# Two small weight loads moved to a second engine's queue, with a new load order and a split copy, in a retention and MLP-mixer kernel

## The chip, the cores and the metric

The kernel runs on one core of a Trainium2 chip. The metric is the device time of one execution in microseconds (us); below, a time is the median of the runs named beside it. Ratios are the mean time of one kernel's fast runs over the mean of the other's fast runs of the same rounds, with a 95% interval, so they are not quite the ratio of the medians that stand beside them. A run is called slow when it took over 1.5% more than the fastest run of the same kernel, and fast otherwise; slow runs are left out of the ratios. Times inside a run count from the start of its profiled span, which is some 2 us shorter than the device time of that execution.

## The reference, cut to what matters

```python
ret = (scale * q @ k.T) * Dmat[None]     # 8 batches, 8 heads, 576 tokens, 64 per head: causal decay
x   = concat_heads(ret @ v)              # [8, 576, 512]
h   = x.transpose(0, 2, 1) @ U @ V       # U [576, 32], V [32, 576]
u   = x + h.transpose(0, 2, 1)
y   = u + relu(u @ w_ch1) @ w_ch2        # 512 -> 2048 -> 512
```

The MLP (the last line) is nearly all of TensorE's work. For the first batch it can only start when attention is done for all tokens, x has gone through U and V, and the first block of `w_ch1` (W1 below) is there as bf16.

## The kernel before

The kernel writes its program with a small planner. Every piece of work is an `op` with engines, an estimated duration, dependencies and a priority. The planner simulates the engines and gives each of them one fixed list of instructions. A load is an op too; the planner estimates its landing with a model of the transfers (`ring`):

```python
            if e == "SP":                                  # an issue on SyncE
                ring = max(ring, t + 700.0) + o.work
                o.vis = ring + self.DMA_LAT                # DMA_LAT = 1700.0: when others may use it
            elif o.work:                                   # an issue on another engine
                ring = max(ring, o.end + 500.0) + o.work
                o.vis = ring + self.DMA_LAT
            else:
                o.vis = o.end + self.LAT[e]
```

The loads of U and V, and their casts to bf16. V [32, 576] is wanted four times, once in each group of 32 partitions, so it is loaded with a broadcast; `VV` also gets a second, shifted copy (`V2`). Staging buffers: `ust`, `vst`.

```python
        def fv(e):
            nc.sync.dma_start(out=vst, in_=moe_V[None, :, :].to_broadcast([4, R, S]))

        ld["lu"] = DMA(1200.0, 500.0, fu, prio=-999.0, after=[ld["consts"]])
        # ...
        ld["lv"] = DMA(500.0, 800.0, fv, prio=-999.0)
        ld["U"] = pl.op("POOL", 250.0, ..., [ld["lu"]], -970.0)
        ld["V"] = pl.op("ACT", 680.0, ..., [ld["lv"]], -935.0, alt=[("DVE", 600.0), ("POOL", 700.0)])
        ld["V2"] = pl.op("POOL", 600.0, ..., [ld["V"]], -150.0)
```

Batch 0's tokens come as two "pairs" of 256 tokens (loads k0 and k2, v0 and v2) and a "half chunk" of 64 tokens (kA, qA, vA). One line fixes the order of the loads on SyncE; the `w` are blocks of the MLP weights:

```python
    line = [...q...] + [load_op(x) for x in ("k0 k2 v0 kA qA v2 vA lu lv w0 w1" + " " + "w2 w3 ...").split()]
```

Where the plan expects TensorE to wait ahead of the MLP, it fills in dummy matmuls on zeros (`ps_big_t<-zer`), which are thrown away.

Of the kernel before, what the change touches and what calls it, by code (L numbers as in the profile page):

```python
# [28 lines left out]
class Plan:  # L29
# [3 lines left out]
    DMA_LAT = 1700.0  # L33
    DMA_AHEAD = 4500.0

# [23 lines left out]
    def run(self, hint=None):  # L59
# [52 lines left out]
        while left:  # L112
            best = None
            for e in engines:
                base = free[e]
                if e == "SP":
                    base = max(base, ring - self.DMA_AHEAD)
                te = INF
                cand = []
                for o, dur in avail[e]:  # L120
                    t = max(base, earliest(o))
                    if t == INF:
                        continue
                    if wary and o.prio > 0 and any(
                        t < (max(hint[h], h.ready)) < t + dur - 150.0 for h in urgent.get(e, ())
                    ):
                        continue
                    cand.append((t, o, dur))
                    te = min(te, t)
                if te == INF:  # L130
                    continue
                t, o, dur = min((c for c in cand if c[0] <= te + self.LOOK.get(e, 1e-6)),
                                key=lambda c: c[1].prio)
                te = t
                k = (te, o.prio)
                if best is None or k < best[0]:
                    best = (k, e, o, dur, te)
# [45 lines left out]
def kernel(  # L183
# [11 lines left out]
    nc = tc.nc  # L195
# [160 lines left out]
    def load_q4(par, prio):  # L356
# [5 lines left out]
        for n, hs in enumerate(halves):  # L362
# [6 lines left out]
            gots.append(DMA(600.0, 3300.0 if par else (1500.0, 2400.0)[1 - n], fn, prio=prio + 0.01 * n,  # L369
# [60 lines left out]
    def load(p, c, prio, early=False, b=None):  # L430
# [17 lines left out]
        for n, (j, dram) in enumerate(((1, k), (0, q), (2, v))):  # L448
# [8 lines left out]
            got[j] = DMA(480.0 if len(pts) == 1 else 900.0, 1220.0 if b is None else 1000.0, fn,  # L457
# [451 lines left out]
    def RV(p, c, prio, q_done=True, b=None, in_sc=False):  # L909
# [49 lines left out]
        def ev_x(e):  # L959
            nc.scalar.activation(out=xs[slot(*xk)][rows].rearrange("p hp hl d -> p hl hp d"),  # L960
                                 in_=po[rows, :, 0:NHP * D].rearrange("p hl (hp d) -> p hl hp d", d=D),
                                 func=AF.Copy)
        if b is None:
            st["x", kb] = [pl.op("DVE", 700.0, ev, [o], prio, rel=[pk])]
        else:
            st["x", kb] = [pl.op("ACT", 610.0, ev_x, [o], prio, rel=[pk])]
# [220 lines left out]
    def load_uv():  # L1187
        gp = nc.gpsimd

        def fu(e):  # L1190
            nc.sync.dma_start(out=ust[:, 0:4, :], in_=moe_U[0:4 * P, :].rearrange("(c p) r -> p c r", p=P))
            nc.sync.dma_start(out=ust[0:HALF, 4, :], in_=moe_U[4 * P:S, :])  # L1192
# [6 lines left out]
        def fv(e):  # L1199
            nc.sync.dma_start(out=vst, in_=moe_V[None, :, :].to_broadcast([4, R, S]))  # L1200

        ld["lu"] = DMA(1200.0, 500.0, fu, prio=-999.0, after=[ld["consts"]])
        ld["lub"] = DMA(1200.0, 500.0, fub, prio=-999.0)
        ld["lv"] = DMA(500.0, 800.0, fv, prio=-999.0)
# [11 lines left out]
    def load_w(prio):  # L1216
        ld["lw"] = []
        for fb in range(4):
            ld["w1", fb] = []
            for hc in range(2):  # L1220
# [8 lines left out]
                o = DMA(450.0, 1400.0 + 350.0 * (fb < 2), fn, prio=prio + fb + hc * 0.1, acq=[key])  # L1229
                ld["lw"].append(o)  # L1230
# [6 lines left out]
        for fb in range(4):  # L1237
            ld["w2", fb] = []
            for hf in range(2):
# [7 lines left out]
                o = DMA(450.0, 1400.0, fn, prio=prio + 10 + fb + hf * 0.1, acq=[key])  # L1247
                ld["lw"].append(o)
# [15 lines left out]
    ld["zero"] = pl.op("POOL", 1600.0, blank, [ld["consts"]], 5.0)  # L1264

    def batch0():
# [4 lines left out]
        for i in range(2):  # L1271
            load_pair(0, i, base + 20 * i, scaled=(2, 2)[i])
# [5 lines left out]
        SC(0, XC, base + 43.0, with_q=False, b=0, apart="sc" == "big")  # L1278
# [92 lines left out]
    line = [ld["q4a", 0], ld["q4", 0]] + [load_op(x) for x in ("k0 k2 v0 kA qA v2 vA lu lv w0 w1" + " " + "w2 w3 w4 w5 w6 w7 w8 w9 q4 w10 w11 kB k5 qB vB v5 k7 w12 w13 w14 w15 lub v7").split()]  # L1371
# [70 lines left out]
```

## Time and profile before

| | before |
|---|---|
| median of 3 runs | 334.8 us (334.13 to 336.29) |
| profiled span, mean TensorE clock | 335.2 us, 0.998 |
| V: issue, landing, first cast | 14.32, 22.36, 22.41 on GpSimd |
| half chunk's k, q and v landed | 13.79, 14.54, 17.47 |
| first real MLP matmul | 24.85 |
| from there to the end | 310.4 us |

The first real MLP matmul is the row `ps_big_t<-uT_t,w_sb` in the timeline. It splits the run into a start, whose limits are loads and hand-overs between engines, and a long part in which TensorE is nearly always at work. The lines that carry this are shown in the prediction.

### The profile page before, as it was taken

Reading aid. Unit: us, or ns where it says so; the run is one execution under the profiler, and the core shown is the slowest. Engines: PE = TensorE matmul, PEld = TensorE weight load, DVE = VectorE, ACT = ScalarE, POOL = GpSimd, SP = SyncE. Lnnn points to the kernel's source line nnn. Section 1 sums busy time; section 2 is a strip of 40 time slices with the busy share of each in tenths; the row PEclk is TensorE's granted clock in tenths of the full one; section 3 lists DMA queues with packets and bytes.
Section 4 is the critical chain, followed back from the end, with each engine's and each line's share of the span. In section 5 each row is a group of like instructions: output and inputs, shape, how many; then the busy total and the mean of one; then the engine's idle time right before and its main releaser. Section 6 shows DMA issues by size and latency. Waiting matters only on the chain.

```text
span 335.2 us, 6423 instructions
## 1 busy us (share of the span) xinstructions
PE 320.2 (96%) x2606; PEld 159.9 (48%) x2649; DVE 154.8 (46%) x243; ACT 134.4 (40%) x240; POOL 87.6 (26%) x123
## 2 busy tenths in 40 slices
PE   8889998999999899999999999999999999999995
PEld 3454445555545444544455454545544444444442
DVE  5843266695755547555467437732533020020011
ACT  4655554468403460166114621364135206404600
POOL 7557447523241213131212321400010010010010
PEclk9999999999999999999999999999999999999999
DMA  8999999998999999999999899942110320011012
GB/s 238 199 277 384 314 222 314 254 243 170 209 227 206 214 195 220 195 230 186 224 218 241 172 208 217 248 73 49 63 65 17 65 93 31 0 65 64 0 47 78
DMA packets 145169, 56.44 MB, mean 168 GB/s; under 512 B 128244, under 2 KB 138484, under 8 KB 145140
## 3 DMA queue, kind: packets, MB, share of 16 engines
q1 hardware_dynamic: 142420, 47.12, 68.1%
q0 software_dynamic: 2720, 8.92, 7.9%
q8 instruction: 20, 0.33, 0.4%
q14 instruction: 9, 0.07, 0.1%
HBM read 37.14 MB, written 9.44 MB: 139 GB/s over the span
## 4 chain that ended last, share of the span: by engine, by line
PE 73%; DMA 12%; SPq 8%; DVE 2%; issue 2%; POOL 1%; ACT 1%
PE ps_big_t L329 63%; DMA q_st<-in_q_dram 5%; DMA st_st<-in_k_dram 5%; SPq L453 4%; PE ps_s L329 4%; PE ps_o L329 3%; PE ps_sc L329 2%; DMA vst<-in_moe_V_dram 2%; SPq L511 1%; DVE ret_t L872 1%; SPq L546 1%; PE ps_big_t L569 1%; SPq L1039 1%; DVE o_sb L1163 1%; SPq L1192 0%
## 5 line engine op out<-in xcount | busy, mean ns | idle before, releaser
L329 PE MATMUL ps_big_t<-uT_t,w_sb 128*128 128x512 bf16 x556 | 131.8, 379 | 1.5 <-POOL w_sb L1233 0.5
L329 PE MATMUL ps_big_t<-w_sb,y_t 128*128 128x512 bf16 x556 | 130.6, 379 | 1.7 <-issue 0.8
L1096 ACT ACTIVATE y_t<-ps_big_t 128x512 bf16<-128x512 f32 x144 | 85.8, 597 | 94.7 <-PE ps_big_t L329 94.0
L329 PEld LDWEIGHTS <-w_sb 128*128 128x128 bf16 x576 | 54.0, 98 | 62.4 <-POOL w_sb L1233 1.1
L329 PEld LDWEIGHTS <-y_t 128*128 128x128 bf16 x576 | 53.9, 98 | 60.6 <-issue 0.8
L1163 DVE TENSOR_TENSOR o_sb<-ps_big_t,u_t 128x512 f32<-128x512 f32 x36 | 24.8, 690 | 82.3 <-PE ps_big_t L329 82.1
L1170 POOL DMA_DIRECT2D out_dram<-o_sb x34 | 19.3, 568 | 136.3 <-DVE o_sb L1163 133.6
L475 POOL TENSOR_TENSOR qkv_t<-st_st,vscale 128x512 bf16<-128x512 f32 (+1 forms) x28 | 29.1, 1040 | 70.2 <-DMA st_st<-in_v_dram 63.8
L872 DVE TENSOR_TENSOR ret_t<-ps_sc,tri 128x1024 bf16<-128x1024 f32 x24 | 29.3, 1220 | 17.1 <-PE ps_sc L329 17.1
L807 ACT ACTIVATE s_sb<-ps_s 128x512 bf16<-128x512 f32 x22 | 13.1, 596 | 55.9 <-PE ps_s L329 55.8
L951 DVE TENSOR_TENSOR x_t<-ps_o,qscale 128x512 bf16<-128x512 f32 x27 | 18.6, 688 | 9.7 <-PE ps_o L329 9.5
L1027 DVE TENSOR_TENSOR u_t<-ps_s,x_t 128x512 bf16<-128x512 f32 x20 | 13.8, 689 | 17.0 <-PE ps_s L329 17.0
L329 PEld LDWEIGHTS <-qkT_t 64*128 64x128 bf16 (+3 forms) x588 | 14.3, 99 | 11.2 <-issue 7.5
L471 DVE CAST qkv_t<-st_st 128x512 bf16<-128x512 f32 x27 | 13.3, 491 | 12.1 <-DMA st_st<-in_k_dram 12.0
L471 DVE CAST qkv_t<-q_st 128x512 bf16<-128x512 f32 x27 | 14.1, 524 | 8.1 <-DMA q_st<-in_q_dram 7.7
L329 PEld LDWEIGHTS <-ret_t 128*128 128x128 bf16 (+2 forms) x336 | 11.4, 97 | 9.3 <-DVE ret_t L872 4.1
L329 PE MATMUL ps_o<-qkv_t,ret_t 128*128 128x64 bf16 (+2 forms) x296 | 11.9, 192 | 2.2 <-DVE ret_t L872 2.1
L329 PE MATMUL ps_sc<-qkT_t 64*128 64x128 bf16 (+2 forms) x336 | 13.3, 215 | 0.7 <-DVE ret_t L872 0.4
L1027 DVE TENSOR_TENSOR u_t<-ps_o,x_t 128x512 bf16<-128x512 f32 x16 | 10.9, 684 | 3.4 <-PE ps_o L329 3.3
L329 PE MATMUL ps_s<-qkv_t 64*64 64x64 bf16 (+2 forms) x188 | 11.3, 206 | 0.4 <-ACT s_sb L678 0.3
L578 ACT ACTIVATE qkT_t<-ps_big_t 128x512 bf16<-128x512 bf16 (+1 forms) x21 | 10.9, 556 | 1.9 <-PE ps_big_t L569 1.5
L329 PEld LDWEIGHTS <-qkv_t 64*64 64x64 bf16 (+2 forms) x220 | 9.0, 105 | 4.9 <-issue 1.5
(112 smaller groups left out, 186.6 us busy)
## 6 DMA issues: line engine op xcount, KB each, us to landing
out_dram<-o_sb POOLq DMA_DIRECT2D x34, 256.0 KB, 3.3
st_st<-in_k_dram SPq DMA_DIRECT2D x24, 256.0 KB, 4.8
q_st<-in_q_dram SPq DMA_DIRECT2D x24, 256.0 KB, 4.9
st_st<-in_v_dram SPq DMA_DIRECT2D x24, 256.0 KB, 5.0
y_t<-in_moe_w_ch_dram SPq DMA_DIRECT2D x10, 512.0 KB, 10.0
wst_t<-in_moe_w_ch_dram SPq DMA_DIRECT2D x6, 512.0 KB, 8.1
st_st<-in_k_dram SPq DMA_DIRECT2D x4, 512.0 KB, 8.7
st_st<-in_v_dram SPq DMA_DIRECT2D x4, 512.0 KB, 8.1
```

The costliest lines, as they stand in the source:

```text
L329: nc.tensor.matmul(*a, skip_group_check=True, **kw)
L453: sent.append(nc.sync.dma_start(out=f[rw, :, :], in_=dram[bb, :, t0:t0 + rw.stop - rw.start, :].rearrange("h s d -> s h d"),))
L471: nc.vector.tensor_copy(**args)
L475: eng.tensor_tensor(out=qkv[slot(*qk)][rows, 2, :, :], in0=at(2)[rows], in1=vscale[rows, c, :, None].to_broadcast([rows.stop - rows.start, ...
L578: nc.scalar.activation(func=AF.Copy, **args)
L807: nc.scalar.activation(out=s_sb[slot(*sk)], in_=ps_s.rearrange("p (a b) -> p a b", b=P), func=AF.Copy)
L872: nc.vector.tensor_tensor(out=ret[slot(*rk)][rows, hl, :, 0:n], in0=bank(hl.start)[rows, None, :, 0:n] if apart else ps_sc[rows, hl, :, 0: ...
L951: nc.vector.tensor_tensor(out=xs[slot(*xk)][rows].rearrange("p hp hl d -> p hl hp d"), in0=po[rows, :, 0:NHP * D].rearrange("p hl (hp d) - ...
L1027: nc.vector.tensor_tensor(out=us[slot(*uk)].rearrange("p (hp hl d) -> p hp hl d", hl=2, d=D), in0=bank().rearrange("p (hp hl d) -> p hp hl ...
L1096: nc.scalar.activation(out=y1s[slot(*yk)][:, f, :], in_=ps_big[slot(*bk)], func=AF.Relu)
L1163: nc.vector.tensor_tensor(out=osb[slot(*ok)], in0=ps_big[slot(*bk)], in1=osb[slot(*ok)] if n else us[slot(*uk)], op=ALU.add)
L1170: eng.dma_start(out=out_flat[row:row + P, :], in_=osb[slot(*ok)])
```

## The change

Its intent: U and V leave SyncE's line of issues and are issued by ScalarE, beside the loads of the first q, so that V lands long before it is wanted; batch 0's k and v pairs all go ahead of the half chunk; the half chunk's output is copied out by ScalarE and VectorE in two halves; GpSimd's zeroing of three tiles moves behind W1's casts. The planner's model of the transfers is adjusted to the new order. The core of the diff:

```diff
-    DMA_LAT = 1700.0
+    DMA_LAT = 2100.0
...
         def fu(e):
-            nc.sync.dma_start(out=ust[:, 0:4, :], in_=...)
-            nc.sync.dma_start(out=ust[0:HALF, 4, :], in_=moe_U[4 * P:S, :])
+            nc.scalar.dma_start(out=ust[:, 0:4, :], in_=...)
+            nc.scalar.dma_start(out=ust[0:HALF, 4, :], in_=moe_U[4 * P:S, :])
...
         def fv(e):
-            nc.sync.dma_start(out=vst, in_=moe_V[None, :, :].to_broadcast([4, R, S]))
-
-        ld["lu"] = DMA(1200.0, 500.0, fu, prio=-999.0, after=[ld["consts"]])
+            nc.scalar.dma_start(out=vst, in_=moe_V[None, :, :].to_broadcast([4, R, S]))
+
+        ld["lu"] = pl.op("ACT", 1300.0, fu, [ld["consts"]], -1999.0, work=200.0)
...
-        ld["lv"] = DMA(500.0, 800.0, fv, prio=-999.0)
+        ld["lv"] = pl.op("ACT", 660.0, fv, (), -1998.0, work=600.0, after=[ld["lu"]])
...
-            st["x", kb] = [pl.op("ACT", 610.0, ev_x, [o], prio, rel=[pk])]
+            insts = []
+            st["x", kb] = [pl.op(e, 390.0, lambda e, hl=hl: ev_x(e, hl, insts), [o], prio, rel=[pk])
+                           for hl, e in enumerate(("ACT", "DVE"))]
...
-    ld["zero"] = pl.op("POOL", 1600.0, blank, [ld["consts"]], 5.0)
+    ld["zero"] = pl.op("POOL", 1600.0, blank, ld["w1", 3], 5.0)
...
-    line = ... "k0 k2 v0 kA qA v2 vA lu lv w0 w1" ...
+    line = ... "k0 k2 v0 v2 kA qA vA w0 w1" ...
```

Cut: a limit on how far SyncE issues ahead (`RING`), names for the weight loads, and two load estimates.

More of the change, by code (lines that the diff above doesn't have):

```diff
@@ L32 @@
     LOOK = {"DVE": 150.0, "ACT": 150.0}
-    DMA_LAT = 1700.0
+    DMA_LAT = 2100.0
     DMA_AHEAD = 4500.0
+    RING = 2900.0
     def __init__(self):
@@ L115, in run @@
                 base = free[e]
-                if e == "SP":
-                    base = max(base, ring - self.DMA_AHEAD)
                 te = INF
@@ L121, in run @@
                     t = max(base, earliest(o))
+                    if e == "SP":
+                        t = max(t, ring - self.DMA_AHEAD if o.name == "w" or ring > 60000.0 else ring + o.work - dur - self.RING)
                     if t == INF:
@@ L368, in fn @@
                 )
-            gots.append(DMA(600.0, 3300.0 if par else (1500.0, 2400.0)[1 - n], fn, prio=prio + 0.01 * n,
+            gots.append(DMA(600.0, 3300.0 if par else (1300.0, 2200.0)[1 - n], fn, prio=prio + 0.01 * n,
                             acq=[] if n else keys))
@@ L456, in fn @@
                     ))
-            got[j] = DMA(480.0 if len(pts) == 1 else 900.0, 1220.0 if b is None else 1000.0, fn,
+            got[j] = DMA(480.0 if len(pts) == 1 else 900.0, 1220.0 if b is None else 1250.0, fn,
                          prio=prio + (0.0, 0.01, 0.5)[n], acq=[] if j == 2 else [home[j]],
@@ L958, in ev, with ev_x @@
             )
-        def ev_x(e):
-            nc.scalar.activation(out=xs[slot(*xk)][rows].rearrange("p hp hl d -> p hl hp d"),
-                                 in_=po[rows, :, 0:NHP * D].rearrange("p hl (hp d) -> p hl hp d", d=D),
-                                 func=AF.Copy)
+        def ev_x(e, hl, insts):
+            args = dict(out=xs[slot(*xk)][rows, :, hl, :],
+                        in_=po[rows, hl, 0:NHP * D].rearrange("p (hp d) -> p hp d", d=D))
+            insts.append(nc.scalar.activation(func=AF.Copy, **args) if e == "ACT" else nc.vector.tensor_copy(**args))
+            if len(insts) == 2:
+                own(insts)
         if b is None:
@@ L1190, in fu @@
         def fu(e):
-            nc.sync.dma_start(out=ust[:, 0:4, :], in_=moe_U[0:4 * P, :].rearrange("(c p) r -> p c r", p=P))
-            nc.sync.dma_start(out=ust[0:HALF, 4, :], in_=moe_U[4 * P:S, :])
+            nc.scalar.dma_start(out=ust[:, 0:4, :], in_=moe_U[0:4 * P, :].rearrange("(c p) r -> p c r", p=P))
+            nc.scalar.dma_start(out=ust[0:HALF, 4, :], in_=moe_U[4 * P:S, :])
         def fub(e):
@@ L1229, in load_w @@
                 o = DMA(450.0, 1400.0 + 350.0 * (fb < 2), fn, prio=prio + fb + hc * 0.1, acq=[key])
+                o.name = "w"
                 ld["lw"].append(o)
@@ L1247, in load_w @@
                 o = DMA(450.0, 1400.0, fn, prio=prio + 10 + fb + hf * 0.1, acq=[key])
+                o.name = "w"
                 ld["lw"].append(o)
@@ L1271, in batch0 @@
         for i in range(2):
-            load_pair(0, i, base + 20 * i, scaled=(2, 2)[i])
+            load_pair(0, i, base + 20 * i, scaled=2)
         load(0, XC, base + 40.0, early=True, b=0)
@@ L1277, in batch0 @@
         t_pe(0, XC, base + 42.0, b=0)
-        SC(0, XC, base + 43.0, with_q=False, b=0, apart="sc" == "big")
+        SC(0, XC, base + 43.0, with_q=False, b=0)
         sp = -4.0
@@ L1370, in load_op @@
         return ld["q4", 1] if x == "q4" else L(x)[0]
-    line = [ld["q4a", 0], ld["q4", 0]] + [load_op(x) for x in ("k0 k2 v0 kA qA v2 vA lu lv w0 w1" + " " + "w2 w3 w4 w5 w6 w7 w8 w9 q4 w10 w11 kB k5 qB vB v5 k7 w12 w13 w14 w15 lub v7").split()]
+    line = [ld["q4a", 0], ld["q4", 0]] + [load_op(x) for x in ("k0 k2 v0 v2 kA qA vA w0 w1" + " " + "w2 w3 w4 w5 w6 w7 w8 w9 q4 w10 w11 kB k5 qB vB v5 k7 w12 w13 w14 w15 lub v7").split()]
     for a, b in zip(line, line[1:]):
```

## The prediction

> **What bounds the kernel now.** I read the page's busy table first, then the chain of work that ended last in order of time, then one-microsecond windows of the first 60 us, then the timeline of the same stretch, and last the DMA records.
>
> ```profile
> PE 320.2 (96%) x2606; PEld 159.9 (48%) x2649; DVE 154.8 (46%) x243; ACT 134.4 (40%) x240; POOL 87.6 (26%) x123
> ```
>
> TensorE is busy for 320.2 of 335.2 us and the change removes none of its real work, so only idle or dummy time of TensorE can be won. Before 24.85 us its busy time is largely dummy matmuls on zeros and small attention pieces; the first real MLP matmul starts at 24.85. The chain leads there:
>
> ```profile
> 12.10 1.00 SPq L1191
> 13.14 1.14 SPq L1192
> 14.32 8.04 DMA vst<-in_moe_V_dram
> 22.41 0.68 POOL VV L1209
> 23.14 0.67 POOL VV L1213
> 23.81 1.00 POOL w_sb L1233
> 24.85 2.76 PE ps_big_t L329 x12
> ...
> 42.90 8.73 DMA st_st<-in_k_dram
> ```
>
> The two U issues hold SyncE's queue for 2.1 us, V takes 8.04 us to land, GpSimd then casts V twice before the first cast of W1, and the first MLP matmul waits for that cast. It looks as if V were the whole startup. The timeline says otherwise:
>
> ```profile
> 20.97 0.59 ACT L960 ACTIVATE x_t<-ps_sc 64x512 bf16<-64x512 f32 x1 [0.25 <-PE ps_sc L329]
> 22.02 0.60 ACT L998 ACTIVATE a_sb<-ps_big_t 128x512 bf16<-128x512 f32 x1 [0.46 <-PE ps_big_t L329]
> 22.41 0.67 POOL L1209 CAST VV<-vst 128x576 bf16<-128x576 f32 x1 [3.21 <-DMA vst<-in_moe_V_dram]
> 23.13 0.38 PE L329 MATMUL ps_big_t<-VV,a_sb 128*128 128x512 bf16 x1 [0.43 <-POOL VV L1209]
> ```
>
> The other operand of the V product, a_sb, is ready at 22.62, against V at 23.08. V costs that path only about 0.46 us: two paths are nearly level. The windows show the third limit, the transfers:
>
> ```profile
> 15.00:16.00 1.00, 0.75 (x33) 0.69 (x33) 0.38 (x1) 0.69 (x2) 0.73 (x1) 1.00 0.86 100
> 16.00:17.00 1.00, 1.00 (x49) 0.79 (x41) 0.64 (x1) 0.82 (x3) 0.59 (x1) 1.00 0.45 81
> 18.00:19.00 1.00, 1.00 (x50) 0.81 (x45) 1.00 (x2) 1.00 (x3) 1.00 (x2) 1.00 0.87 199
> 25.00:26.00 1.00, 1.00 (x6) 0.40 (x5) 0.72 (x2) 0.00 (x0) 0.94 (x1) 1.00 1.05 387
> 50.00:51.00 1.00, 0.60 (x25) 0.54 (x27) 0.97 (x2) 0.00 (x0) 1.00 (x2) 1.00 1.08 367
> 51.00:52.00 1.00, 0.57 (x24) 0.38 (x20) 1.00 (x2) 0.35 (x1) 0.61 (x2) 1.00 1.08 383
> ```
>
> The last two columns are the DMA share and GB/s. From 3 to 42 us the share is about 1 or above except at 15 to 19, around U and V, where 81 to 232 GB/s flow instead of the 387 that W1 gets at 25. In the rows at 50 and 51 TensorE (first pair) is busy for 0.60 and 0.57 of each us: it waits there for batch 1, whose k lands at 51.63 as the chain shows. So the transfer line, not the start at 24.85 alone, decides where TensorE stands at 55 us. Summing TensorE's busy time by 5 us windows, it idles 2.1 us between 40 and 55, and another 1.5 us between 110 and 120.
>
> **What the skill says.** "DMA: Bandwidth & Descriptors", section "Rules for kernel authors", says that a transfer whose outermost dimension is a broadcast of c copies runs on at most c engines. V's is a broadcast of four. The trace agrees: V's 128 packets of 2304 B run from 15.72 to 21.21, about 5.5 us for 288 KB, and its last four semaphore increments come at 21.96 to 22.36 while no others arrive near them. W1's first block shows the same four behind: twelve increments by 21.01, four at 23.28 to 23.52. The same page, "Issuing engines are not separate DMA queues", says that issuing from another engine saves only the issuing time; the transfers share the 16 engines. Its "Queues, rings and completion order" says each engine takes turns between queues packet by packet. Before has a single hardware queue (142420 packets on q1), so no line shows the sharing yet. "PSUM — Partial Sum Buffer", section "PSUM bank collisions raise a hardware error", lets ScalarE and VectorE read different banks together. The half chunk's output lies in two banks, and the trace has such a pair already (18.91 on ScalarE, 19.23 on VectorE).
>
> **The change part by part.**
>
> 1. U and V move to ScalarE's queue. Their issue follows the constants: the last trix activation ends at 3.65. Two U issues at 0.50 and 0.58 (the uncongested pair at 49.2 us) and V at 0.66 end near 5.5. ScalarE has nothing else before 7.62, so nothing waits. SyncE gets back 1.00 + 1.14 + 0.66 = 2.8 us of issuing, which produced the hole at 15 to 17 us. Lost transfer in that hole: (1 - 0.86) + (1 - 0.45) = 0.7 us.
>
> 2. V's bytes don't go away. In packets of 93 ns, as at 16.7 to 17.3 where it ran alone, 32 packets on each of four engines are 3.0 us; at the 178 ns it averaged beside W1 (22.3 us of packets over 128) they are 5.6. U is 576 packets at 15 ns over 16 engines, 0.5 us. Both now lie ahead of k and v on those four engines, and a load is done only when its slowest engine is. I take 2.7 us of delay for batch 0's loads: 3.5 less about 0.8 that another engine was late anyway (k lands at 8.43 where fifteen engines were done at 7.93; v at 12.56 where they were done at 11.75).
>
> 3. Order k k v v. The second v (16.34 before) goes ahead of the half chunk's k and q, whose landings cost 14.54 - 12.56 = 2.0 us: it would land at 14.4 + 2.7 = 17.1. The half chunk's q lands about 2 us after that, at 19.1. From there I add the durations of the same work in before: q scale 1.04, transposes and copy 0.8, scores and mask 1.1, its output matmuls 0.9, copy 0.4, last U product 0.4, and 0.5 of hand-overs = 5.1. So a_sb would start at about 24.2 against 22.02. The first MLP matmul then follows with no wait for V: a_sb 0.60, V product 0.45, copy 0.65, about 0.2 of hand-overs: 26.1 instead of 24.85. With V costing nothing it would be 23.4. I take 25.6 as my middle, as ports and packets may overlap better than a plain sum.
>
> 4. The half chunk's copy in two: 0.59 becomes about 0.4 (the 64x256 pair at 18.91 and 19.23 took 0.36 and 0.43), 0.2 us won; already counted in the 5.1.
>
> 5. The zeroing on GpSimd, 0.95 + 0.52 + 0.52 = 2.0 us at 4.0 to 5.9, moves behind W1. GpSimd can cast q at 4.7 instead of 5.96. That wins 0.4 us on q, but k lands later than q is ready, so nothing is left of it. It later fits GpSimd's idle stretch at 36.8 to 40.6.
>
> 6. The transfer line behind: on the four engines V still stands before W1's first block, so that one is earlier only by the hole, 0.7 us, and by whatever V runs faster than its 5.6 us, at most 2.6. I take 1.2 us. W1's block lands near 22.3 and its cast, with V's casts long done, is ready at 23.4, before it is needed.
>
> **The sum.** The start of the MLP goes from 24.85 to about 25.6 (0.8 later). Batch 1's loads come 1.2 earlier. TensorE had 2.1 us of waiting in 40 to 55; the later start uses up 0.8 of it and the earlier loads remove 1.2, leaving about 0.1. At 55 us TensorE is then about 1.2 us ahead. Behind 55 both TensorE and the transfers have moved by the same 1.2, so most carries through; I take 0.4 off for waits on orders of transfers at 100 to 120 that don't move along. Gain 0.8: 334.8 - 0.8 = 334.0 us.
>
> **Rivals.** (a) V early is nearly free, as the queues interleave: the MLP starts at 23.4 to 24 and the transfers are 2.6 ahead. For it: V's packets took 93 ns alone. Against: packets of 2304 B slowed W1 to 199 GB/s at 18. It would make 332.3. (b) V early holds the four engines for 5.6 us and SyncE, which is held back when any engine is behind (its v issue at 3.40 took 2.66 us), stalls too: the MLP starts at 27.5 or later, past what the 2.1 us of slack absorbs. For it: the spread of V's packets beside other traffic. It would make 336. (c) A new plan: the latency (2100 for 1700) and the ring model change the order of every engine's instructions, so parts after 60 us may move by 1 us either way. For it: the waits at 110 to 120 are for orders (SyncE's transposes and loads behind VectorE). Nothing in the profile gives its sign. (d) All is hidden and the time is the same within 0.3 us: the loads after 60 us have a DMA share above 1 to 200 us.
>
> **Range and chances.** The sum lies between rivals (a) and (b), whose ends are 332.3 and 336.0, and the three runs of before spread by 2.2 us. I take 332.1 to 335.9 for 8 in 10. Two per cent are 6.7 us; the whole removable startup (24.85 to 23.4) plus the waits in 40 to 55 and 110 to 120 is 1.5 + 2.1 + 1.5 = 5.1. So faster by 2% is nearly excluded (0.02), slower takes a broken order (0.02), and 0.96 is left.
>
> **What would show it.** Step 1: a second hardware queue in the table of queues, and no hole at 15 to 17. Step 2: V landing by 9 to 12 us, k and v later than 8.43 and 12.56 by up to 3 us. Step 3: the wait ahead of the first MLP matmul names ScalarE's or VectorE's uT, not GpSimd's w_sb. Step 6: W1's first cast before 23.5 and batch 1's k before 51. It would be wrong if V's landing doesn't delay k at all, or if TensorE still waits 2 us between 40 and 55, or if the difference sits after 100 us.

## The result, and the profile after

| | before | after |
|---|---|---|
| median | 334.91 us (4 runs, 334.13 to 336.29) | 345.07 us (4 runs, 344.51 to 345.76) |
| ratio of the fast runs | | 1.030 [1.026, 1.034]: slower |
| profiled span, clock | 335.2 us, 0.998 | 344.1 us, 0.978 |
| V: issue, landing, first cast | 14.32, 22.36, 22.41 | 8.75, 19.92, 19.95 |
| half chunk's k, q and v landed | 13.79, 14.54, 17.47 | 20.24, 20.95, 21.25 |
| first real MLP matmul | 24.85 | 37.04 |
| from there to the end | 310.4 us | 307.0 us |

The kernel came out about 10 us slower, and the prediction (334.0 us, 332.1 to 335.9, "slower" at 0.02) was wrong. All of the loss is in the start: the first MLP matmul comes 12.2 us later, and 3.4 us of that come back afterwards. They come from waits of TensorE that before had: between the first MLP matmul and 62 us it idles 2.2 us before and 0.7 after, between 100 and 150 us 2.4 before and 0.6 after, together 3.3. (Between 62 and 100 us it idles 0.9 us more after, so this account is rough.)

From the page of after, the busy line, two rows of the 40 slices (one digit for 8.6 us, tenths busy or tenths of the clock) and the second hardware queue:

```profile
PE 325.5 (95%) x2614; PEld 162.3 (47%) x2657; DVE 155.0 (45%) x243; ACT 133.3 (39%) x240; POOL 89.1 (26%) x125
...
PE   8559999899999999999999999999999999999995
...
PEclk9659999999999999999999999999999999999999
...
q10 hardware_dynamic: 740, 0.37, 0.6%
```

The second hardware queue, q10, is there with U's and V's 740 packets. TensorE and its clock both dip in the second and third slice (8.6 to 25.8 us), where before has 8 and 8 and a full clock. The same stretch as windows, TensorE's busy time first, then weight loads, VectorE, ScalarE and GpSimd; the last three columns are the granted clock, the DMA share and GB/s. Before:

```profile
10.00:15.00 5.00, 3.92 (x83) 2.07 (x82) 4.52 (x5) 2.70 (x6) 2.92 (x4) 1.00 1.29 212
15.00:20.00 5.00, 4.75 (x174) 3.99 (x174) 2.77 (x5) 3.14 (x7) 3.54 (x4) 1.00 0.85 172
```

After:

```profile
10.00:15.00 5.00, 3.17 (x46) 2.17 (x47) 1.45 (x2) 2.75 (x7) 0.88 (x2) 0.63 1.25 248
15.00:20.00 5.00, 1.31 (x5) 0.35 (x3) 1.33 (x2) 0.06 (x1) 0.00 (x0) 0.50 1.11 202
```

From 15 to 20 us three engines stand still at once: TensorE runs 5 matmuls instead of 174, ScalarE nothing, GpSimd nothing. The transfers don't: their share rose from 0.85 to 1.11, so the hole of before was filled as intended. Something waits, and not for bandwidth. The chain of work that ended last, in order of time (start, duration, what), names it:

```profile
1.86 6.87 DMA st_st<-in_k_dram
8.73 0.02 issue
8.75 11.17 DMA vst<-in_moe_V_dram
19.92 0.02 issue
19.95 0.68 ACT VV L1216
20.63 0.49 ACT qkT_t L579
21.12 0.04 issue
21.17 0.64 PE ps_o L330 x13
```

In before the chain went from V to the MLP directly. Here it goes from V's landing to V's cast on ScalarE, and from there to `qkT_t`, a piece of attention that has nothing to do with V: the copy of the second pair's transposed k. Two things that share only an engine have become a chain. The timeline shows how (start, duration, engine, line, operation; in brackets the idle time before it and what ended it):

```profile
8.75 1.11 ACTq L1205 DMA_DIRECT2D vst<-in_moe_V_dram  x1
...
9.91 1.21 ACT L423 ACTIVATE qkT_t<-ps_sc 128x256 bf16<-128x256 bf16 x4 [6.26 <-DMA ust<-in_moe_U_dram]
...
12.16 0.62 ACT L525 ACTIVATE qkv_t<-st_st 128x512 bf16<-128x512 f32 x1
...
19.95 0.68 ACT L1216 ACTIVATE VV<-vst 128x576 bf16<-128x576 f32 x1 [7.17 <-DMA vst<-in_moe_V_dram]
...
20.69 0.67 POOL L1218 COPY VV<-VV 128x576 bf16<-128x576 bf16 x1 [8.42 <-ACT VV L1216]
...
21.17 0.64 PE L330 MATMUL ps_o<-qkT_t 64*64 64x128 bf16 x16 [4.63 <-ACT qkT_t L579]
...
21.32 3.05 POOL L530 TENSOR_TENSOR qkv_t<-st_st,vs 128x512 bf16<-128x512 f32 x3
```

ScalarE stands for 7.17 us ahead of V's cast, from 12.78; behind it wait the copies of the second pair's transposed k, which TensorE had finished by 15.3. GpSimd stands for 8.42 us ahead of V's second copy, with v's casts (`L530`) behind it, whose first data had landed at 12.89. And the first bracket is a second finding: ScalarE copies the transposed q only at 9.91 (7.62 in before), right after it has issued V. The profile's releaser there (U) is only the last event that it saw; the program's list tells more. ScalarE's instructions in the program's order, with the semaphores they wait for:

```
L1196 DMACopy ust<-in_moe_U_dram 128x4x32 [waits DVE]
L1197 DMACopy ust<-in_moe_U_dram 64x32 [waits DMAHW0]
L1205 DMACopy vst<-in_moe_V_dram 128x1x576 [waits DMAHW2]
L423 Activation qkT_t<-ps_sc 128x256 [waits PE] x4
L525 Activation qkv_t<-st_st 128x512
L579 Activation qkT_t<-ps_big_t 128x512 [waits PE]
L525 Activation qkv_t<-st_st 128x512 [waits DMAHW3]
L1216 Activation VV<-vst 128x576 [waits DMAHW2]
L579 Activation qkT_t<-ps_big_t 128x512 [waits PE] x2
```

The loads of SyncE and ScalarE share eight semaphores (DMAHW0 to 7), and V got the one that the first k was using. So V's *issue* waits until that k has landed: it landed at 8.73 and V was issued at 8.75. The same pair in four of the experiments below: 8.21 and 8.23, 8.12 and 8.14, 8.63 and 8.66, 8.15 and 8.17. An engine that issues a load can be held by another load's landing. (The trace holds the same: V's issue waits for the semaphore that the first k's landing counts up.)

Why is V's cast where it is? Because the planner believed in an early V. Its own figures for after (in us of the plan, whose k0 lands at 8.2 against 8.73 in the trace) and what the trace has:

```
                     plan          trace
V issued             5.69          8.75
V landed            10.99         19.92
V's cast            11.03         19.95
first MLP matmul    24.78         37.04
```

3.1 us of the 8.9 that the landing is late come from the issue, the rest from a flight of 11.17 us where the plan has 5.3.

### The profile page after: what moved, and what is told of

It reads as the page before. It is cut to its first block, busy times and chain, and to the rows that moved or that the text cites. A ratio compares the mean times of both kernels' runs of the same rounds, so it can differ in the third digit from the quotient of the medians.

```text
span 344.1 us, 6434 instructions
## 1 busy us (share of the span) xinstructions
PE 325.5 (95%) x2614; PEld 162.3 (47%) x2657; DVE 155.0 (45%) x243; ACT 133.3 (39%) x240; POOL 89.1 (26%) x125
## 4 chain that ended last, share of the span: by engine, by line
PE 87%; DMA 7%; DVE 2%; issue 1%; SPq 1%; ACT 1%; DVEq 0%
PE ps_big_t L330 72%; PE ps_o L330 5%; PE ps_s L330 5%; PE ps_sc L330 4%; DMA vst<-in_moe_V_dram 3%; DMA st_st<-in_k_dram 2%; DMA q_st<-in_q_dram 2%; PE ps_big_t L570 1%; SPq L1044 1%; DVE o_sb L1168 1%; DVE ret_t L873 1%; DVE ret_t L717 0%; ACT qkT_t L579 0%; SPq L366 0%; PE ps_sc L405 0%
## 5 line engine op out<-in xcount | busy, mean ns | idle before, releaser
L873 DVE TENSOR_TENSOR ret_t<-ps_sc,tri 128x1024 bf16<-128x1024 f32 x24 | 29.3, 1222 | 20.7 <-PE ps_sc L330 20.6
L330 PEld LDWEIGHTS <-qkT_t 64*128 64x128 bf16 (+3 forms) x588 | 15.0, 104 | 16.8 <-issue 7.9
L472 DVE CAST qkv_t<-st_st 128x512 bf16<-128x512 f32 x27 | 14.0, 518 | 4.6 <-DMA st_st<-in_k_dram 4.5
L330 PE MATMUL ps_big_t<-zer 128*128 128x512 bf16 x30 | 11.5, 523 | 1.5 <-DVE zer L279 1.3
```

Of the source, the lines that this page charges most:

```text
L330: nc.tensor.matmul(*a, skip_group_check=True, **kw)
L472: nc.vector.tensor_copy(**args)
L873: nc.vector.tensor_tensor(out=ret[slot(*rk)][rows, hl, :, 0:n], in0=bank(hl.start)[rows, None, :, 0:n] if apart else ps_sc[rows, hl, :, 0: ...
```

## The experiments

Three theories were on the table. **A, order**: V's cast and second copy stand in ScalarE's and GpSimd's lists ahead of work whose data is there, and everything behind them waits for V. **B, engines**: V's broadcast on four of the DMA engines delays every load that also uses those four, the half chunk's above all. **D, clock**: TensorE's halved clock from 11.3 to 24.9 us makes the start slow. The new load order and ScalarE's blocked issue are smaller suspects. "First MLP" below is the time of the first real MLP matmul in the profiled run; the kernels ran on several chips, each beside runs of before on the same chip, whose medians lay between 334.5 and 336.0. Each is compared by its ratio to those.

### V's casts late, all else as in after

```diff
         RV(0, XC, base + 59, q_done=False, b=0, in_sc=True)
+        ld["V"].after.extend(st["x", (XC, 0)])
+        ld["V2"].after.extend(st["x", (XC, 0)])
```

> The changed kernel, with one edit: the program order puts the casts of V behind the half chunk's output instead of ahead of batch 0's second k pair; the load of V stays on ScalarE's queue, at the same place. Theory A (in-order blocking: the 10 us come from ScalarE and GpSimd standing still for V's landing at 19.9, with V's cast ahead of work whose data had landed): ScalarE's 7.2 us wait before L1216 goes, TensorE's pause from 16.5 to 21.2 goes, the first MLP matmul moves from 37.0 to about 28 and the time falls from 345 to about 337. Theory B (transfer contention: V on four engines beside the loads delays k and v, and the cast's place hardly matters): k of the half chunk still lands near 20.2 and the time stays at 342 or more. V should land near 19.9 under both.

Measured: 338.85 us, ratio 1.016 [1.006, 1.026], first MLP at 30.51. V still lands at 19.87 and the half chunk's k at 20.18. The long waits on ScalarE and GpSimd for V are gone and the clock is 1.0 throughout the profiled run. This lies between the two forecasts (337 and 342 or more), nearer to A's. In the first 30 us the order of instructions differs from after's, on all engines but TensorE, in these two casts alone; TensorE's gets a few other dummies. How much comes back depends on how it is counted: 6.2 of 10.2 us by the medians (345.07, 338.85 and 334.91, which come from different sessions), 1.4 of 3.0 per cent by the ratios, 6.5 of 12.2 us by the first MLP matmul. Theory A is about half of the loss, perhaps more. What holds the start now is in the chain that ended last:

```profile
8.23 1.11 ACTq L1205
9.38 1.21 ACT qkT_t L423 x4
...
19.70 1.79 issue
```

It begins with the first k's landing, V's blocked issue on ScalarE and q's copy behind it, at 9.38 (7.62 in before), and goes on through attention to TensorE, which then stops for 1.79 us in the middle of a group of matmuls; for this stop the profile shows no releaser, and its cause stays open. GpSimd does wait 4.7 us for the half chunk's k, but its cast is done by 20.85 and TensorE comes to that k only at 22.01: B is not on this chain.

### V alone back on SyncE; U stays on ScalarE

```diff
-            nc.scalar.dma_start(out=vst, ...)
+            nc.sync.dma_start(out=vst, ...)
-        ld["lv"] = pl.op("ACT", 660.0, fv, (), -1998.0, work=600.0, after=[ld["lu"]])
+        ld["lv"] = DMA(500.0, 800.0, fv, prio=-999.0)
-    "k0 k2 v0 v2 kA qA vA w0 w1"
+    "k0 k2 v0 v2 kA qA vA lv w0 w1"
```

> The changed kernel with V alone back on SyncE's queue, behind the half chunk's v; U stays on ScalarE's queue, and all the rest of the change stays. Theory A and B both expect most of the loss to go, as neither the cast nor the transfer of V is then in the way: half chunk's k lands near 16 instead of 20.2, first MLP matmul near 25, time 334 to 336. Theory C (the new order k k v v, or the new constants of the plan, cost it): time stays above 340. It also shows what U alone costs on ScalarE's queue.

Measured: 336.03 us, ratio 1.006 [0.998, 1.014], first MLP at 26.87, half chunk's k at 16.02, V's cast on VectorE at 21.70. Much as expected (the first MLP 1.9 us later than the 25 that was forecast): with everything else of the change kept, the loss is gone but for what the interval can't tell from zero. The half chunk's k lands 4.2 us earlier than with V in flight beside it (20.18 and 20.24): that is how much B delays this load. It is not what B costs in time, as this edit also ends the blocked issue: ScalarE copies q at 7.30 instead of 9.38. No run separates the two.

### U and V back on SyncE

```diff
-        ld["lu"] = pl.op("ACT", 1300.0, fu, [ld["consts"]], -1999.0, work=200.0)
+        ld["lu"] = DMA(1200.0, 500.0, fu, prio=-999.0, after=[ld["consts"]])
   (V as above; the line "... vA lu lv w0 w1")
```

> The changed kernel with U and V both back on SyncE's queue where they were; order k k v v, half copies, zeroing behind W1 and the plan's constants stay. Theories A and B: 334 to 336, within 0.5% of before, as the remaining parts move nothing on the path. Theory C (those remaining parts cost the 10 us): 343 or more.

Measured: 338.61 us (336.8 to 340.7), ratio 1.013 [1.004, 1.023], first MLP at 30.45. Higher than expected, a miss in part. V lands at 21.77 and its cast was planned on ScalarE ahead of the copies of x, with a wait of 2.3 us: theory A again, smaller. The profiled run also shows something in the clock column of its windows:

```profile
16.00:19.80 3.80, 3.03 (x89) 2.27 (x85) 2.48 (x4) 2.22 (x5) 2.25 (x3) 1.00 1.02 220
19.80:25.00 5.20, 4.70 (x54) 2.37 (x46) 1.28 (x2) 1.18 (x2) 2.39 (x3) 0.50 1.04 335
25.00:30.00 5.00, 5.00 (x32) 2.62 (x30) 0.50 (x2) 1.55 (x3) 3.78 (x5) 0.50 1.05 383
```

TensorE runs at half clock from 19.8 to 30.0 in this run, though after its first matmul it is nowhere idle for over 0.6 us before. That this is the rest of the loss isn't shown: the runs of this kernel with mean clocks 0.985, 1.0, 0.997 and 0.987 took 338.71, 338.51, 336.79 and 340.71 us, so the one at full clock is no faster than the profiled one.

### The move of U and V alone, on before

```diff
 (before, with the changed fu, fv, ld["lu"] and ld["lv"] of the change, and)
-    "k0 k2 v0 kA qA v2 vA lu lv w0 w1"
+    "k0 k2 v0 kA qA v2 vA w0 w1"
```

> The kernel before with the move of U and V to ScalarE's queue alone; order k k v, half chunk, v and all constants as before. Theory A: the plan again believes that V lands early and puts its cast on ScalarE ahead of the half chunk's k, so ScalarE waits some 5 us for V: 341 to 346. Theory B: 341 to 346 too, as the transfers overlap in the same way. Theory C (order or constants are needed for the loss): 334 to 337.

Measured: 337.13 us (335.6 to 340.3), ratio 1.007 [0.998, 1.017]; the profiled run is the slowest, 340.32, with its first MLP at 32.4. A miss: I expected most of the loss. V lands at 18.09 here, and in the plan with before's constants, which puts V's cast later, ScalarE's wait for it is 4.3 us instead of 7.2. It seems that the cost of a misplaced cast depends on how far the list has got when the wait comes; no run varies that alone.

### Dummy matmuls in TensorE's two pauses

```diff
+    warm = {id(tpe[1]): 8, id(scp[2]): 18}     # TensorE's pieces behind the two pauses
...
                 zeros(at + 40.0, o.start - 80.0)
+                for _ in range(warm.get(id(o), 0)):
+                    mm(ps_s, zer[:, 0:P], zer, start=True, stop=True)
```

> The changed kernel with 26 more dummy matmuls on zeros, 8 ahead of the transposes that wait at 9.8 us and 18 ahead of the scores that wait at 16.5 us; nothing else moves. It asks what the halved clock of TensorE (0.5 from 11.3 to 24.9 us) costs by itself. If the halved clock matters (theory D): clock 1.0 through 30 us, first MLP matmul 1.5 to 3 us earlier than 37.0 and the time about 342.5 to 343.5. If it is only a mark of the waiting (theory A alone): clock 1.0, but the first MLP matmul within 0.7 us of 37.0, time 344 to 345.5.

Measured: 345.78 us, ratio 1.033 [1.023, 1.043], first MLP at 38.1. Its windows:

```profile
10.00:15.00 5.00, 4.74 (x60) 2.46 (x59) 2.46 (x4) 2.66 (x7) 0.88 (x2) 1.00 1.25 244
15.00:20.00 5.00, 3.22 (x15) 1.27 (x13) 0.38 (x1) 0.06 (x1) 0.00 (x0) 1.00 1.14 190
20.00:25.00 5.00, 3.84 (x39) 1.69 (x40) 3.05 (x3) 1.60 (x3) 4.31 (x5) 0.57 0.86 277
```

The clock is 1.00 up to 20 us where after has 0.63 and 0.50, and the time is the same within the intervals, a little above both forecasts. D falls for the pauses: the half clock there is a by-product of the waiting. It halved later, from 20.7 to 27.5, which this run didn't prevent.

### V as the very first issue on ScalarE, its casts late

```diff
-        ld["lv"] = pl.op("ACT", 660.0, fv, (), -1998.0, work=600.0, after=[ld["lu"]])
+        ld["lv"] = pl.op("ACT", 660.0, fv, (), -2001.0, work=600.0)
   (and V's casts late, as in the first experiment)
```

> The changed kernel with the load of V as the very first issue on ScalarE's queue (so it meets no earlier load on its semaphore, and flows beside the first q as the change's name says) and the casts of V behind the half chunk's output, as in the run with late casts (338.85, first MLP matmul 30.5, half chunk's k at 20.2). Semaphore theory (E: V's issue at 8.75 waited for the landing of the first k because both use one semaphore): V is issued near 0.8 and lands by 7, and ScalarE copies q near 7.6 to 8 instead of 9.9. If then the half chunk's k lands near 17 and the first MLP matmul is near 27: 335 to 336.5, contention only matters where V collides with the half chunk. If V on four engines delays all behind it wherever it flows (theory B): k of the half chunk still near 19 to 20 and 338 or more.

Measured: 343.38 us, ratio 1.027 [1.019, 1.034], first MLP at 33.84. The chain of waits now begins

```profile
0.81 10.10 DMA vst<-in_moe_V_dram
```

and the DMA records show B directly. A load counts up its semaphore once for each engine that is done. For q's second half twelve of the sixteen counts are in by 7.75 and the last four come at 11.16 to 11.56; for the first k twelve by 10.83, four at 12.76 to 13.11; for the second k twelve by 12.36, four at 14.48 to 14.88. In before q's second half was whole at 6.15. V, alone on four engines, delays these loads on those four by 2 to 4 us, and takes 10 us itself even when it is first. Not all of this run's time is B, though: U's issue (10.99) waited for V's landing (10.91) on a shared semaphore, U landed at 17.90, and its cast stood on GpSimd ahead of the second k's, whose data had been there since 14.88; TensorE waits 1.8 us for that.

### V as four loads of 32 rows, on the kernel with V on SyncE

```diff
-            nc.sync.dma_start(out=vst, in_=moe_V[None, :, :].to_broadcast([4, R, S]))
+            for i in range(4):
+                nc.sync.dma_start(out=vst[32 * i:32 * i + 32, :], in_=moe_V)
```

> The run with V back on SyncE (336.0; V issued at 12.5, landed at 21.7, last four increments of W1's first block 2 us behind) with one edit: V as four loads of 32 rows each in place of one broadcast. Theory B in its narrow form (the broadcast runs on four engines): sixteen engines carry V, it lands within 5 us of its issue, near 18, W1's first block lands near 20.5 instead of 22.8 with its increments together, and all of W1 comes 1.5 to 2 us earlier. The time then falls only if the start of the MLP was waiting for transfers: 334 to 336. Rival: the four issues and their semaphores cost SyncE as much as they win, W1 no earlier than 22.5.

Measured: 336.38 us (one of four runs slow, which is the profiled one), ratio 1.005 [0.995, 1.015]. W1's first block lands at 20.64 (22.78 with the broadcast), its sixteen counts together but one. That block came earlier as expected, but V's last piece landed only at 19.61 (near 18 was expected) and the next blocks of W1 hardly earlier than with the broadcast (23.56 against 24.11, 25.18 against 25.46); the time did not move.

### The old load order in after

```diff
-    "k0 k2 v0 v2 kA qA vA w0 w1"
+    "k0 k2 v0 kA qA v2 vA w0 w1"
```

> The changed kernel with the old order of loads (k k v, half chunk's k and q, then the second v); U and V stay on ScalarE's queue. If the order k k v v is innocent: V's cast still stands ahead of the second k pair's copies on ScalarE, time 343 to 346. If the order matters (the move alone, on before, cost only 2 us): 336 to 340.

Measured: 343.2 us, ratio 1.028 [1.018, 1.038], first MLP at 33.89, ScalarE's wait for V 6.0 us. Beside after's 1.030 the order k k v v costs nothing that can be told from noise. The medians differ by 1.9 us and the first MLP by 3.2, so a cost of that size isn't excluded either.

### V first, as four loads of 32 rows, its casts late

```diff
   (the kernel with V first, and)
-            nc.scalar.dma_start(out=vst, in_=moe_V[None, :, :].to_broadcast([4, R, S]))
+            for i in range(4):
+                nc.scalar.dma_start(out=vst[32 * i:32 * i + 32, :], in_=moe_V)
```

> The run with V issued first (343.4; q's second half late on four engines by 4 us, half chunk's k at 21.8) with one edit: V as four loads of 32 rows in place of the broadcast. Narrow theory B (what hurts the loads is that the broadcast runs on four engines): V lands by 6, q's second half by 7.5 with its increments together, half chunk's k by 17.5, first MLP matmul near 27.5 instead of 33.8, time 335 to 337.5. Rival (any V beside the first loads delays them, as its bytes have to pass): q's second half still after 9 and the time 341 or more.

Measured: 343.86 us, ratio 1.025 [1.020, 1.029], first MLP at 33.44. B's delays are gone: q's second half is whole at 7.31 with its counts together, V's last piece lands at 9.01 in the trace and the half chunk's k at 16.66. The time is a miss all the same. The table of waits says why:

```profile
POOL UU L1211 <- DMA ust<-in_moe_U_dram: 5.1, 1, 5.1
PE ps_big_t L570 <- POOL qkv_t L527: 4.8, 1, 4.8
```

U is now issued behind V's four pieces, at 7.39, because that issue again waits for a semaphore (q's second half, landed at 7.31), and it lands at 13.9; its cast stands in GpSimd's list ahead of the second k pair's (`L527`). GpSimd waits 5.1 us for U, TensorE 4.8 us for GpSimd. The same fault with another tile. So neither this run nor the one with V as four loads on SyncE shows that B cost device time: both took B's delays away and neither became faster (in this one the wait for U may hide it).

### The same four loads, on before

Two kernels: before with V as four loads of 32 rows on SyncE, and before with those four as the first issues on ScalarE (casts where the planner puts them).

```diff
+            for i in range(4):
+                nc.sync.dma_start(out=vst[32 * i:32 * i + 32, :], in_=moe_V)        # first kernel
+                nc.scalar.dma_start(out=vst[32 * i:32 * i + 32, :], in_=moe_V)      # second kernel
```

> The kernel before with one edit: V as four loads of 32 rows on SyncE's queue, at V's old place. From the run with the same edit on V back on SyncE, where W1's first block landed at 20.6 instead of 22.8: W1's first block lands near 21 instead of 23.5, batch 1's k near 49.5 instead of 51.6, and TensorE's 2.2 us of waiting between its first MLP matmul and 62 us shrinks to about 1. The first MLP matmul moves little (24.3 to 24.9), as a_sb is ready only at 22.6. Time 1 to 2.5 us below before. Rival: the semaphores and issues eat it, within 0.3%.

> The kernel before (its order, its constants, U where it was) with V as four loads of 32 rows issued first on ScalarE's queue. What the change wanted, with sixteen engines: V lands by 6, q and k are later by at most 1 us, V's casts are done by 7.5 and W1's first block lands near 21.5. Time 332.5 to 334.5. Rival: ScalarE's four issues (about 1.6 us) delay the constants and V's cast stands ahead of q's copies on ScalarE and GpSimd, so all starts 1 us or more later: 335 to 338.

Measured: the first 336.72 us (333.3 to 340.1, two of six runs slow), ratio 1.002 [0.997, 1.007], the same. A miss: 1 to 2.5 us were to be won. Its profiled run is the fastest of its six, with W1's first block at 20.36, the first MLP at 22.91 and a span of 330.9 us, but the other runs don't follow. The second, a miss too: 339.01 us, ratio 1.010 [1.007, 1.014], first MLP at 29.31: V's cast on ScalarE at 8.79 and its second copy on GpSimd stand ahead of q's casts, and TensorE pauses from 6.71 to 10.83.

### V first in four loads, and U's cast late too

In the kernel with 1.025, one instruction moves: U's cast on GpSimd, from ahead of the second k pair's cast to behind the half chunk's.

```diff
         ld["V2"].after.extend(st["x", (XC, 0)])
+        ld["U"].after.append(st["v", 3])
```

> The kernel with V in four pieces first on ScalarE and V's casts late, and now also U's first cast moved, on GpSimd alone, from ahead of the second k pair's cast to behind the second v pair's and the half chunk's k cast; it is the one instruction that moves. If what was left of the loss there is again a cast placed in an engine's order ahead of work whose data has landed (the in-order theory), the 5.1 us wait of GpSimd and the 4.8 us wait of TensorE for it go, the first MLP matmul comes at 27 to 29 instead of 33.4, and the time is 335 to 338 against 343.9. If an early V costs the time in another way (the transfers, the clock), the first MLP matmul stays above 31.5 and the time at 341 or more. Below 334 would show that the move can be made to win.

Measured: 337.63 us (5 runs), ratio 1.007 [1.002, 1.013], first MLP at 28.49. Both waits are gone, and with them 5 us of the start; the ratio went from 1.025 to 1.007 (each beside before on its own chip). As forecast, and this is A in its purest form: the two traces hold the same instructions in the same order on every engine, but for this one cast. (The two kernels ran on different chips, each beside before.) What ScalarE does early is still held up, as the head of this kernel's chain shows:

```profile
1.84 7.77 DMA vst<-in_moe_V_dram
...
9.63 0.53 ACTq L1197
...
10.20 1.21 ACT qkT_t L423 x4
```

V's third piece landed at 9.61, U's second issue (`L1197`) waited for that semaphore until 9.63, and q's copy on ScalarE, at 7.62 in before, came at 10.20: the blocked issue, once more.

### The rest: without the plan's dummies

That kernel's first MLP is still 3.6 us later than before's. From 12.1 us on its chain has no transfer in it, almost only TensorE's own list, and the plan has put 16 dummies there (6 in the same stretch of before). Is that list what costs the 3.6 us? Three kernels leave out the dummies behind the first pair's: this one, the one with V on SyncE, and before as a control.

```diff
-        for _ in range(min(n, 14)):
-            mm(bank, zer[:, 0:P], zer, start=start, stop=True)
+        for _ in range(min(n, 14, 20 - len(fill))):        # 21 and 22 in the other two
+            fill.append(mm(bank, zer[:, 0:P], zer, start=start, stop=True))
```

> The kernel with V in four pieces first and all casts late, without the 16 dummy matmuls on zeros that its plan places behind the first k pair's transposes (from 12.3 us of its trace). If the rest of the loss is TensorE's own list (16 dummies at 0.22 to 0.38 us), the first MLP matmul comes 2.5 to 3.5 us earlier, at 25 to 26 instead of 28.5, and the time is 333.5 to 336, level with before or a little ahead of it. If the rest is the transfers (the half chunk's q at 18.8 against 14.5), the waits reappear where the dummies were, the first MLP matmul moves by less than 1 us and the time stays near 337. A third way: with the pauses unfilled the granted clock halves for some us, and the time is above 338.

> The kernel with V alone back on SyncE, without the 14 dummies that its plan places from 12.4 us on. Its first MLP matmul was at 26.9 and its time 1.006 of before. If TensorE's list sets it, 24.5 to 25.5 and 333 to 335; but there V's own landing, at 21.7, and its cast come close behind, so less is to be won than in the run with V first: if they set it, 26 or later and 335 to 336.

> Control: before without its last dummies (6 in the trace from 11.6 us on). Its start waits for V and W1's first cast at 22.4 to 24.9, not for TensorE, so nothing should be won: first MLP matmul at 24.5 to 25, time within 0.5% of before. If the time gets worse by more, the dummies keep the clock up there.

Measured: 337.61 us, ratio 1.007 [1.002, 1.012], first MLP at 28.64; 339.74 us, 1.012 [1.007, 1.018], 30.72; 335.71 us, 1.001 [0.996, 1.005], 24.52. The dummies cost nothing: without them TensorE of the first kernel idles 7.0 us before its first MLP matmul instead of 4.1, and starts no earlier. In the first kernel's chain

```profile
4.22 9.72 DMA st_st<-in_v_dram
...
14.09 2.05 POOL qkv_t L530 x2
```

a load is in it again, the first v, which lands at 13.95 against 12.56 in before; the half chunk's k, q and v land at 17.29, 18.26 and 19.04 against 13.79, 14.54 and 17.47. So the rest goes with later loads, as V's, U's and the second v's bytes now lie ahead of the half chunk; how much of it is the blocked ScalarE these runs don't tell. The second kernel, a miss, is slower where its clock halves (from 19.9 to 33.6 in the profiled run): its five runs fall into two with mean clock 1.0 (337.13 and 336.62) and three with 0.975 to 0.978 (339.7 to 341.3). With the dummies its four runs all had 0.998 to 1.0, and without them some runs of the other two kernels too show a lower clock than with them (0.97, in a slow run, and 0.985 are the lowest). The dummies may thus keep the clock up, but the chips differ and no run tests it.

## Why the prediction was wrong

**Step 1 failed: "ScalarE has nothing else before 7.62, so nothing waits."** V's issue was to end near 5.5; it ended at 9.86, because it waited for the first k's semaphore, and ScalarE, which was to copy q at 7.62, stood behind it until 9.91. In after the wait for V hides what this costs; in the run with V's casts late, where that wait is gone, it heads the chain (q's copy 1.8 us late). I had asked what ScalarE does, not what the issue itself may wait for. The second half of the step held: the hole in the transfers at 15 to 20 us is filled.

**The step that is missing: where V's cast stands.** Step 6 says "with V's casts long done" and nothing more. No step asks where the planner would put the casts once it believes V to be early, nor what happens if V is late. The Trainium skill has the fact that decides it: "PSUM — Partial Sum Buffer", section "Engine vs sequencer instructions", says that the queues of ScalarE, VectorE and GpSimd are strictly first in, first out. The trace agrees: ScalarE stands for 7.17 us and GpSimd for 8.42, with work behind them whose data was there by 15.3 and 12.89. The diff has the planner's belief in plain sight: `work=600.0` and a latency of 2.1 us for a load whose flight in before had been 8.04. Moving the two casts gave half of the loss back or somewhat more (338.85 us, ratio 1.016); moving U's cast alone took the other kernel from 1.025 to 1.007. In before the fault couldn't show: V landed at 22.36, and nothing of batch 0's attention was left to stand behind it.

**Step 2 was right in kind and mis-sized.** V's four engines do delay the other loads: 4.2 us for the half chunk's k (20.24 against 16.02 with V on SyncE), where I took 2.7 for batch 0's loads. And it hit other loads than I said. The first v landed only 0.3 us later (12.89 against 12.56), since V was not yet in flight; V "landing by 9 to 12" was 19.92. V's flight is the term that was mis-sized, 10 to 11 us instead of 3.0 to 5.6, and not by the pace of its packets: they took 171 ns on average and ran from 12.69 to 18.90, near to the 5.6. What the step leaves out is the time around them: 3.9 us from the issue to the first packet (1.4 in before) and 1.0 us from the last packet to the landing. With the late issue these make up the delay.

**Step 3** had `a_sb` at about 24.2; it came at 35.30. With V out of the way (V on SyncE) it is 25.13, and with V first and all casts late 26.75, so the sum of durations itself was 1 to 2.5 us short, not 11.

**Steps 4 and 5 held.** The half copies ran at once, both at 34.05, one on each of the two banks, and took 0.38 us on ScalarE and 0.42 on VectorE against 0.59 for the whole; and the zeroing, now at 35.7 to 37.6, shows up in no wait of TensorE. **Step 6** had W1's first block at 22.3, and it landed at 22.54; its cast, predicted ready at 23.4, began only at 27.34, because GpSimd was 7 to 8 us behind in its list. That did no further harm, as the MLP started at 37. The "2.1 us of slack" behind the start, and the 1.5 at 110 to 120, were real: most of the 3.4 us that came back were absorbed there.

**Of the rivals**, (b) named V's hold on the four engines and put the time at 336; the run that has it, and the blocked issue, without the misplaced casts took 338.85. (c), a new plan, was held to 1 us either way "after 60 us"; it was the part that the runs have shown, and it struck before 22 us. The chance of 0.02 for "a broken order" was far too low for a change that lets a planner with wrong constants reorder five engines.

**What stays open.** The sizes of the two kernels with U and V on SyncE or moved alone (ratios 1.013 and 1.007 where 1.00 and 1.03 were expected) mix planned order with half-clock windows that differ from run to run; I can't split them. That a shared semaphore held the issues rests on the program's lists and on times that fall together in every run looked at (five pairs for V, and U's 7.31 and 7.39, 9.61 and 9.63); no run removed that wait alone. What B costs in time is open too: V on SyncE took it away only together with the blocked issue. No version was shown to beat before.

Some readings in the prediction are off, and nothing rests on them: V's packets in before averaged 174 ns (22.3 us over 128), not 178, and U's 17, not 15; and other counts do arrive near V's last four, those of W1's second block from 22.13.

## What to carry to other kernels

When a load moves, follow its consumer: find where the cast or copy that uses it will stand in its engine's list, and what stands behind it, because an early place with a late landing stops an engine whose other data is there. A consumer that isn't urgent is put as late as its own user allows; here that was two lines and half of the loss or more. Before an issue is given to an engine that computes, look at what the issue waits for, and before a small load is put in front, count the DMA engines it runs on.

## What the Trainium skill lacked or had wrong

- "DMA: Bandwidth & Descriptors", "Issuing engines are not separate DMA queues", counts only the issuing time when a load is issued elsewhere. It lacks that the issue can stop the engine that computes: V's, of 1.11 us, waited for another load's landing in a program whose loads share eight semaphores (8.73 and 8.75, and four more such pairs), and held ScalarE until 9.86.
- The same page, "Rules for kernel authors", has that a leading broadcast confines a load to as many engines; the runs agree (V's semaphore counts up one by one four times, at 19.06, 19.18, 19.56 and 19.92). It lacks the cost for the neighbours: the last four counts of the loads behind it came 2 to 4 us after the other twelve, and the load itself took 10.1 us when it was the first. Four loads of 32 rows cured that (q's second half at 7.31 instead of 11.56).
- "TensorE: Matmul & The Clock Gate", "What's actually happening", ties the half clock to an idle window of about 3.4 us. In the kernel with U and V on SyncE it halved for 10.2 us after a stretch of 3.8 us with 3.03 busy and no pause over 0.6 us since its first matmul, and one and the same program had it in three of five runs. The page says of the first change of clock that its moment varies from run to run, and tells further down of one kernel in which frequent short pauses brought it about; it gives no size or number of such pauses, and so no way to tell from a list of instructions whether it will halve.
